# Eight weight chunks instead of six converted beside attention, and one conversion stage of the MLP less

## The chip, the cores and the metric

The kernel runs on one core of one Trainium2 chip. The metric is device time in microseconds (us). Each time comes from one execution; a kernel is timed several times, and one further execution is recorded by the hardware profiler. The engines work side by side, each through its own instructions in their order: PE (TensorE: matmuls, and PEld, its weight loads), DVE (VectorE), ACT (ScalarE), POOL (GpSimd), and SP (SyncE), whose queue issues most DMAs.

## The reference

The program is attention with a causal mask and a decay bias, followed by a block that mixes tokens by a Fourier transform and ends in an MLP. Cut to what matters:

```python
# q, k, v: 8 batches x 8 heads x 576 tokens x 64; s: 8 x 8 x 576
scores = scale * np.matmul(q, k.transpose(0, 1, 3, 2))
cum = np.cumsum(np.maximum(s, 0.0), axis=-1)
bias = -(cum[:, :, :, None] - cum[:, :, None, :])
scores = np.where(causal, -1e9, scores + np.minimum(bias, 0.0))
attn = softmax(scores)
x = heads joined(attn @ v)                      # 8 x 576 x 512
u = x + np.real(np.fft.fft(np.fft.fft(x, axis=1), axis=2))
un = (u - mean(u)) / np.sqrt(var(u) + 1e-6)
out = u + np.maximum(un @ w_ch1, 0.0) @ w_ch2   # 512 x 2048, 2048 x 512
```

The two weight matrices arrive as 64-bit floats, seen by the kernel as pairs of 32-bit words. They have to be rounded to 32-bit floats on the chip, and are then split into a high and a low part, since a product is made of three matmuls on such parts.

## The kernel before

**Attention.** The loop in fused_kernel runs over 32 head pairs i (8 batches of 4 pairs). In iteration i several generators are woven together by weave, which always goes on with the stream that has the least of its total behind it: scores(i) (matmuls of L491 and L492, exponentials of L495 on ACT), av(i - 1) (attention times values, L523), maxes(i + 1), and loads, casts and the finishing of other pairs. maxes(i + 1) is a chain that comes back to PE: low writes the low part of k on DVE (L435), matmuls on L459 write pm, ten reductions on DVE (L466, two helped by L462) leave the row maxima in Mx, PE transposes Mx (L471), ACT copies it, and a DMA puts it into KQ, from which scores(i + 1) starts. The pm tiles and the results of av share five PSUM buffers.

From the second half of each fourth pair on, folds and fourier run for the batch that has been finished, woven into the next batch's attention. The last batch's transform runs inside the first part of the MLP.

**Weights.** There are 16 chunks f of 128 x 1024 weights. A chunk is converted in four quarters by rounded: a DMA of 256 KB brings raw (L78), DVE takes exponent and mantissa apart (L83, L85), ACT shifts the exponent (L84), DVE puts in the sign and the low bits (L87, L88), POOL multiplies the two (L89). The first NC = 6 chunks are converted beside attention by convert_w, which keeps one set of buffers and writes each quarter (128 KB) to DRAM as wD. In each iteration the stream take(weights, share) may go on by share, where a quarter costs 0 + 0.4 + 0.4 + 0.2 by its yields; take stops after the step that reaches the share. For chunks below NC, load_w later reads all 512 KB from wD into wl (L107), copies wl to wh on ACT (L112), and subtracts (L114: the first half on DVE, the second on POOL). For the other chunks load_w converts on the spot, in buffers of a pool named stage.

**MLP.** The 4608 tokens are nine tiles of 512. mlp_tile runs over the chunks: twelve matmuls make h (L183), ACT and DVE make zh and zl of it (L187, L188), and twelve matmuls add the chunk before into acc (L196 to L198). All weights stay in SBUF, so only the first tile waits for them. They come from the generator rest: chunks 3 to 7 into pool w1, converted in stage1 (4 sets of buffers) where they aren't in wD; then it runs the last batch's fourier to its end, closes the pool of the Fourier tables, and in its memory opens wB and stage2 (3 sets) for chunks 8 to 15. The stream ahead draws from rest as the first tile goes on, and mlp_tile draws from it when a chunk two ahead is missing.

**Order.** In attention and its tail the order on PE is the order of the program text (manual_schedule), up to order.close() before the MLP. All else is put in order by a scheduler.

Of the kernel before, what the change touches and what calls it, by code (L numbers as in the profile page):

```python
# [24 lines left out]
NF = FF // 128  # L25
NEG = -1.0e30
TOK = 512
NC = 6
NC1 = 4.5
N0 = 3  # L30
N1 = 8
WEXP = 0x38000000 + (20 << 20)
# [9 lines left out]
def fused_kernel(ctx, tc, qkT, vA, sP, wP, tabD, tabS, corr, out):  # L42
# [3 lines left out]
    NP = NB * 4  # L46
# [27 lines left out]
    def rounded(pool, f, x, bufs):  # L74

        m = pool.tile([128, WC], I32, tag="wm", name="wm", bufs=bufs)
        raw = pool.tile([128, 2 * WC], I32, tag="raw", name="raw", bufs=bufs)
        nc.sync.dma_start(out=raw, in_=wP[f, :, WC * x:WC * x + WC].bitcast(I32))  # L78
        hi = raw.rearrange("p (n w) -> p n w", w=2)[:, :, 1]
        lo = raw.bitcast(U16).rearrange("p (n w) -> p n w", w=4)[:, :, 1]  # L80
        yield 0.0
        e = pool.tile([128, WC], I32, tag="we", name="we", bufs=bufs)
        nc.vector.tensor_scalar(e, hi, 0x7FF00000, None, op0=ALU.bitwise_and)  # L83
        nc.scalar.activation(e, e, AF.Relu, bias=wbias, scale=8.0)  # L84
        nc.vector.tensor_scalar(m, hi, 0xFFFFF, 0x100000, op0=ALU.bitwise_and, op1=ALU.bitwise_or)  # L85
        yield 0.4
        nc.vector.scalar_tensor_tensor(out=e, in0=hi, scalar=-0x80000000, in1=e, op0=ALU.bitwise_and, op1=ALU.bitwise_or)  # L87
        nc.vector.scalar_tensor_tensor(out=m.bitcast(F32), in0=lo, scalar=2.0 ** -16, in1=m, op0=ALU.mult, op1=ALU.add)  # L88
        nc.gpsimd.tensor_mul(e.bitcast(F32), m.bitcast(F32), e.bitcast(F32))  # L89
        yield 0.4  # L90
        return e.bitcast(F32)

    def convert_w(pool, lo, hi, bufs):

        for f in range(lo, hi):
            for x in range(1024 // WC):
                m = yield from rounded(pool, f, x, bufs)
                nc.sync.dma_start(out=wD[f, :, WC * x:WC * x + WC], in_=m)
                yield 0.2

    def load_w(pool, f):
# [3 lines left out]
        W[f] = (wh, wl)  # L105
        if f < NC:
            nc.sync.dma_start(out=wl.bitcast(F32), in_=wD[f])  # L107
        n = 512 if f < NC else WC
        for x in range(1024 // n):
            xs = slice(n * x, n * x + n)  # L110
            m = wl[:, xs].bitcast(F32) if f < NC else (yield from rounded(stage, f, x, nstage))
            nc.scalar.copy(wh[:, xs], m)  # L112
# [287 lines left out]
    def load(i):  # L400
        b, j = divmod(i, 4)
        qk = atop.tile([128, 2, S], F32, tag="qk", name="qk", bufs=3)
        nc.sync.dma_start(out=qk, in_=qkT[b, j])
        kq = KQ[i % NR]
        sts[i] = dict(b=b, j=j, qy=kq[:, 1], ky=kq[:, 0, :, 0:S], kq=kq, qk=qk)
# [100 lines left out]
    def av(i):  # L506
        st = sts[i]
        va = st["va"]
        x = attb.tile([128, S], F32, tag="stage", name="stage", bufs=3)
        r1 = rows[32 + 32 * (i % 2):33 + 32 * (i % 2)]  # L510
        sums = attb.tile([32, 36], F32, tag="sums", name="sums", bufs=2)
        for h in range(2):
            P = st["P"][h]
            vs = slice(64 * h, 64 * h + 128)
            for lo, n, tg in ((0, 256, "A"), (256, 320, "B")):
                p = psm.tile([128, 512], F32, tag="m", name="pav" + tg, bufs=5)
                cs = [c for c in range(5) if CH[c][3] < lo + n]
                for c in cs:
                    qk = CH[c][3]
                    a = max(lo, qk)  # L520
                    o = POFF[c] + a - qk
                    w = lo + n - a
                    nc.tensor.matmul(p[:, a - lo:n], va[:, c, vs], P[:, o:o + w], start=c == 0, stop=c == cs[-1])  # L523
                    if c == cs[-1]:
                        if h:
                            nc.scalar.copy(r1[:, lo:lo + n], p[0:1, :n])
                            nc.scalar.copy(x[64:128, lo:lo + n], p[64:128, :n])  # L527
                        else:
                            nc.scalar.copy(x[:, lo:lo + n], p[:, :n])
                    yield 4 * w / 2.4  # L530

            nc.sync.dma_start(out=sums[16 * h:16 * h + 16], in_=r1 if h else x[64:65])
        st.update(x=x, sums=sums)
# [41 lines left out]
    mixing = None  # L575
    weights = convert_w(attb, 0, NC, 1)
    tiles = [(t, min(TOK, NT - t)) for t in range(0, NT, TOK)]
    stage_ctx = ExitStack()

    def pool(name, **kw):  # L580
        return tc.tile_pool(name=name, bufs=1, reuse_waits="tile", **kw)
# [3 lines left out]
    for i in range(NP):  # L585
        if i + 3 < NP:
            load(i + 3)
        streams = []
        if i >= 1:
            streams.append([av(i - 1), AV * (0.95 if i % 4 == 1 else 1.0)])  # L590
        if 2 <= i + 1 < NP:
            streams.append([maxes(i + 1), MAXES / 0.7])
            streams.append([later(low(i + 1), i % 4 == 0), (6, 7, 4, 3)[i % 4]])
        if 3 <= i + 2 < NP:
            streams.append([high(i + 2), 6])
        if i == 2:
            load_tables()
        if i >= 2:
            streams.append([later(call(recip, i - 2), 4), 10])
            streams.append([later(call(finish, i - 2), 6), 10])  # L600
        if i >= 6 and i % 4 == 2:
            b = (i - 6) // 4
            folding = folds(b, *xbuf[b])
            streams.append([later(take(folding, 5), 2), 7 / 0.7])
        if i >= 7 and i % 4 == 3:
            streams.append([folding, FOLDS - 5])
        if mixing is not None:
            quota, pace = MIX[i % 4]
            streams.append([take(mixing, FOURIER * quota), FOURIER * pace])
        share = NC1 * 4.0 / (NP - 2) if i < NP - 2 else (1.0, 4.0)[i - NP]  # L610
        streams.append([take(weights, share), share + 1e-9])
        if i == NP - 1:
            atop_ctx.close()
            lnp = ctx.enter_context(pool("lnp"))
            mlps = [ctx.enter_context(pool("mlp0"))]
            norm = ln_tile(*tiles[0], 6)
            streams.append([take(norm, 10), 10 / 0.9])
        streams.append([scores(i), SCORES * (1.1 if i % 4 == 1 else 1.0)])
        weave(*streams)
        if i >= 7 and i % 4 == 3:  # L620
            mixing = fourier(b, *xbuf.pop(b))
# [5 lines left out]
    stage, nstage = attb, 1  # L627
# [5 lines left out]
    weave([folds(b, *xbuf[b]), 1.0])  # L633
    mixing = fourier(b, *xbuf.pop(b))
    attb_ctx.close()
    stage, nstage = stage_ctx.enter_context(pool("stage1", side="right")), 4
    w1 = ctx.enter_context(pool("w1"))
    accp = ctx.enter_context(pool("accp", space=PSUM))
    order.close()
# [56 lines left out]
def later(gen, n):  # L696
    for _ in range(n):
        yield 1.0
    yield from gen
# [113 lines left out]
```

## Time and profile before

| | us |
|---|---|
| three timed runs | 1424.47, 1429.97, 1430.12 (median 1429.97) |
| profiled execution, its own time | 1426.1 |
| its span, from the first to the last instruction | 1424.4 |
| PE busy | 1305.1 (92%) |
| DVE busy | 745.7 (52%) |
| POOL busy | 561.6 (39%) |
| ACT busy | 539.3 (38%) |
| mean granted clock of TensorE | 0.971 |

How to read the profile: the page gives busy times of the engines over the span and a chain of waits. A table by stretches cuts the span into pieces and gives, for each, its limits and length, then the busy time of PE, PEld, DVE, ACT and POOL with the number of instructions as (xN), then granted clock, DMA share and GB/s. A group of instructions has line, engine, operation, output<-input, shape and count, then busy time and mean ns of one, then the idle time of its engine before them and what ended it. A timeline row has start and duration in us, engine, line, operation, and in square brackets how long the engine had been idle and who released it. PE's recorded matmuls overlap, so a busy PE isn't yet a PE at its peak.

### The profile page before, as it was taken

What the parts mean: (1) busy time and instruction counts of PE and PEld (TensorE: products, weight loads), DVE (VectorE), ACT (ScalarE), POOL (GpSimd) and SP (SyncE); (2) the same over time, 40 slices, a digit from 0 to 9 for tenths busy, and PEclk for the clock granted to TensorE, in tenths of its full rate; (3) what the DMA queues carried; (4) which work ended last, traced back from release to release, by engine and by line L of the source; (5) the groups of instructions that cost most, each with busy time, mean ns of one, the idle gap of its engine ahead of it and who ended that gap; (6) DMA issues with size and microseconds to landing.
All of it is one profiled execution on the core that took longest, in us unless ns stands there. A gap on an engine that the chain in (4) does not pass through costs nothing.

```text
span 1424.4 us, 17997 instructions
## 1 busy us (share of the span) xinstructions
PE 1305.1 (92%) x6190; PEld 1068.7 (75%) x6190; DVE 745.7 (52%) x1684; ACT 539.3 (38%) x1211; POOL 561.6 (39%) x543
## 2 busy tenths in 40 slices
PE   4887979897988887997899999999999999999998
PEld 3766868686777676775688888888888888888886
DVE  6667677877777788799833233222332223322212
ACT  4775756676665656344321121211212112121110
POOL 6445465656546566565720402204022040123300
PEclk9998999999999997999899999999999999999999
DMA  8555556565655555433200000000000000000000
GB/s 214 156 159 144 163 149 180 158 168 159 159 161 144 166 149 163 162 123 121 79 8 30 31 30 15 15 30 31 30 15 15 30 30 30 15 16 0 30 0 30
DMA packets 78230, 125.05 MB, mean 88 GB/s; under 512 B 11256, under 2 KB 36249, under 8 KB 78139
## 3 DMA queue, kind: packets, MB, share of 16 engines
q1 hardware_dynamic: 75627, 119.83, 28.4%
q0 software_dynamic: 1696, 2.50, 0.9%
q10 hardware_dynamic: 816, 1.57, 0.3%
q8 instruction: 49, 0.80, 0.2%
q14 instruction: 42, 0.34, 0.1%
HBM read 76.85 MB, written 23.07 MB: 70 GB/s over the span
## 4 chain that ended last, share of the span: by engine, by line
PE 51%; DVE 7%; POOL 2%; DMA 1%; issue 1%; ACT 1%; SPq 0%; DVEq 0%; POOLq 0%; ACTq 0%
PE h L183 25%; PE acc L198 8%; PE acc L196 8%; PE acc L197 8%; POOL we L89 1%; DVE wm L88 1%; DVE we L83 1%; DVE wm L85 1%; DVE we L87 1%; DVE wl L114 1%; ACT wh L112 1%; DMA wl<-wD 0%; POOL wl L114 0%; DVE ucl L148 0%; DVE zl L188 0%
## 5 line engine op out<-in xcount | busy, mean ns | idle before, releaser
L188 DVE SCALAR_TENSOR_TENSOR zl<-h,zh 128x512 fp32r<-128x512 f32 x144 | 98.6, 686 | 405.5 <-ACT zh L187 405.4
L187 ACT ACTIVATE zh<-h 128x512 fp32r<-128x512 f32 x144 | 85.9, 596 | 530.1 <-PE h L183 530.1
L198 PE MATMUL acc<-zl,wh 128*128 128x512 f32 x576 | 227.5, 396 | 4.9 <-DVE zl L188 4.9
L196 PE MATMUL acc<-zh,wh 128*128 128x512 f32 x576 | 227.6, 395 | 1.0 <-ACT zh L187 1.0
L197 PE MATMUL acc<-zh,wl 128*128 128x512 f32 x576 | 226.8, 394 | 0.0
L523 PE MATMUL pavB<-P,va 128*128 128x320 f32 (+2 forms) x640 | 189.1, 389 | 9.5 <-ACT stage L527 8.9
L459 PE MATMUL pm<-KQ 128*128 128x256 f32 (+3 forms) x384 | 156.5, 427 | 44.4 <-DVE Mx L466 23.1
L495 ACT ACTIVATE P<-ps 128x320 f32<-128x320 f32 (+4 forms) x384 | 145.9, 393 | 110.5 <-PE ps L492 106.8
L491 PE MATMUL ps<-KQ 128*128 128x256 f32 (+2 forms) x384 | 154.1, 404 | 24.4 <-ACT P L495 14.0
L183 PE MATMUL h<-uch,wh 128*128 128x512 f32 x576 | 159.9, 398 | 8.3 <-ACT wh L112 8.3
L183 PE MATMUL h<-uch,wl 128*128 128x512 f32 x576 | 158.1, 396 | 0.8 <-DVE wl L114 0.8
L183 PE MATMUL h<-ucl,wh 128*128 128x512 f32 x576 | 156.9, 393 | 0.0
L466 DVE CUSTOM_DVE_ANT_0 trash<-pm,amask 128x128 bf16<-128x128 f32 (+3 forms) x256 | 123.5, 482 | 34.2 <-PE pm L459 16.9
L212 POOL TENSOR_TENSOR o<-o,w 128x512 f32<-128x512 f32 x32 | 41.8, 1305 | 252.3 <-issue 218.5
L183 PEld LDWEIGHTS h<-uch,wh 128*128 128x128 f32 x576 | 108.2, 190 | 35.9 <-ACT wh L112 12.1
L198 PEld LDWEIGHTS acc<-zl,wh 128*128 128x128 f32 x576 | 108.7, 189 | 32.0 <-DVE zl L188 6.9
L183 PEld LDWEIGHTS h<-uch,wl 128*128 128x128 f32 x576 | 109.2, 190 | 26.6 <-DVE wl L114 1.2
L196 PEld LDWEIGHTS acc<-zh,wh 128*128 128x128 f32 x576 | 108.6, 188 | 26.1 <-ACT zh L187 1.8
L183 PEld LDWEIGHTS h<-ucl,wh 128*128 128x128 f32 x576 | 108.9, 189 | 24.7
L197 PEld LDWEIGHTS acc<-zh,wl 128*128 128x128 f32 x576 | 108.6, 189 | 24.7
L459 PEld LDWEIGHTS pm<-KQ 128*128 128x128 f32 x384 | 78.4, 207 | 64.7 <-DVE Mx L466 30.2
L492 PE MATMUL ps<-q,k 128*128 128x256 f32 (+2 forms) x384 | 120.5, 316 | 3.1 <-POOL q L438 3.1
(140 smaller groups left out, 2066.9 us busy)
## 6 DMA issues: line engine op xcount, KB each, us to landing
qk<-in_qkT_dram SPq DMA_DIRECT2D x32, 576.0 KB
raw<-in_wP_dram SPq DMA_DIRECT2D x64, 256.0 KB
va<-in_vA_dram SPq DMA_DIRECT2D x32, 480.0 KB
q<-KQ SPq DMA_DIRECT2D x32, 288.0 KB
k<-KQ SPq DMA_DIRECT2D x32, 288.0 KB
rb<-rd SPq DMA_DIRECT2D x64, 144.0 KB
u<-uD SPq DMA_DIRECT2D x8, 1024.0 KB
out_dram<-o SPq DMA_DIRECT2D x32, 256.0 KB
```

The source lines that it names most:

```text
L183: nc.tensor.matmul(h[:, :n], a[:, j * 128:(j + 1) * 128], b[:, j, :n], start=i == 0, stop=i == 11)
L187: nc.scalar.activation(zh[:, :n], h[:, :n], AF.Relu)
L188: nc.vector.scalar_tensor_tensor(out=zl[:, :n], in0=h[:, :n], scalar=0.0, in1=zh[:, :n].bitcast(F32), op0=ALU.max, op1=ALU.subtract)
L196: nc.tensor.matmul(acc[j][:, :n], a[:, cs], y[:, :n], start=g == 0, stop=False)
L197: nc.tensor.matmul(acc[j][:, :n], b[:, cs], y[:, :n], start=False, stop=False)
L198: nc.tensor.matmul(acc[j][:, :n], a[:, cs], z[:, :n], start=False, stop=g == NF - 1)
L459: nc.tensor.matmul(p[:, :n], qy[:, h, 128 * c:128 * c + 128], ky[:, h, k0:k0 + n], start=True, stop=True)
L466: nc.vector.tensor_tensor_reduce(out=trash[:nq, :n], in0=p[:nq, :n], in1=amask[:nq, m0:m0 + n], scale=1.0, scalar=first if x else NEG, op0 ...
L491: nc.tensor.matmul(p[:, :n], ky[:, h, ksl], qy[:, h, a:a + n], start=True, stop=False)
L492: nc.tensor.matmul(p[:, :n], k1[:, h, ksl], q1[:, h, a:a + n], start=False, stop=True)
L495: nc.scalar.activation(P[:, o:o + a + n - lo], p[:, lo - a:n], AF.Exp, scale=0.125)
L523: nc.tensor.matmul(p[:, a - lo:n], va[:, c, vs], P[:, o:o + w], start=c == 0, stop=c == cs[-1])
```

## The change

NC goes from 6 to 8, so chunks 6 and 7 are also converted beside attention and read from wD. Up to pair 6 the share is 1.6 a pair; in pairs 7 to 29 it is 4.0 * 4 / (30 - 7) = 0.696 (before, 4.5 * 4 / 30 = 0.6 in all of pairs 0 to 29); the shares of the last two pairs stay 1.0 and 4.0. Nothing is left to convert in w1, so stage1 goes.

```diff
-NC = 6
-NC1 = 4.5
+NC = 8
+NEARLY = 7
+NC1 = 4.0
...
-        share = NC1 * 4.0 / (NP - 2) if i < NP - 2 else (1.0, 4.0)[i - NP]
+        share = (1.6 if i < NEARLY else NC1 * 4.0 / (NP - 2 - NEARLY)) if i < NP - 2 else (1.0, 4.0)[i - NP]
         streams.append([take(weights, share), share + 1e-9])
...
     attb_ctx.close()
-    stage, nstage = stage_ctx.enter_context(pool("stage1", side="right")), 4
+    stage, nstage = None, 0
     w1 = ctx.enter_context(pool("w1"))
```

One line is added near the top, so lines of the changed kernel are one higher from there on (L466 becomes L467).

On DVE, in the fourth head pair of attention, the maxima of pair 4 stood in one piece before (k is the low part of k, trash and Mx belong to the maxima, sums to another pair's row sums):

```order
L435 TENSOR_TENSOR k_670<-qk,KQ_120 64x576 x2
L466 ISA trash,Mx_128<-pm,amask 128x128
L466 ISA Mx_128 128x1
L466 ISA trash,Mx_128<-pm,amask 128x256
L466 ISA Mx_128 128x1
L466 ISA trash,Mx_128<-pm,amask 128x384
L466 ISA Mx_128 128x1
L466 ISA trash,Mx_128<-pm,amask 128x512
```

At the same place two quarters of a chunk (we, wm and raw are their tiles) now stand among them:

```order
L436 TENSOR_TENSOR k_710<-qk,KQ_120 64x576 x2
L467 ISA trash,Mx_128<-pm,amask 128x128
L467 ISA Mx_128 128x1
L84 TENSOR_SCALAR we<-raw 128x256
L86 TENSOR_SCALAR wm<-raw 128x256
L89 SCALAR_TENSOR_TENSOR wm<-raw,wm 128x256
L88 SCALAR_TENSOR_TENSOR we<-raw,we 128x256
L467 ISA trash,Mx_128<-pm,amask 128x256
...
L84 TENSOR_SCALAR we<-raw 128x256
L86 TENSOR_SCALAR wm<-raw 128x256
L467 ISA trash,Mx_128<-pm,amask 128x512
```

The maxima behind them move back by four and by eight instructions. The pattern is the same in the pairs around it; from pair 7 on there is one quarter a pair, after three to five maxima, and from pair 26 on none.

On PE, at the start of the first token tile, the last batch's transform (pzc, pzs, pyc, pys and p) came in pieces between the chunks, and its last matmul stood behind chunk 5 (wh_6615):

```order
L183 MATMUL h<-uch,wh_6615 128x512 x4
L183 MATMUL h<-uch,wl_6616 128x512 x4
L183 MATMUL h<-ucl,wh_6615 128x512 x4
...
L284 MATMUL pzs<-dsin_81,Do_6509 96x256
...
L336 MATMUL p_6968<-scos_83,z_92 4x290
L183 MATMUL h<-uch,wh_6622 128x512 x4
```

Now all of it but its first six matmuls stands in one piece between chunk 3 and chunk 4 (wh_6664):

```order
L293 MATMUL pzc<-dcos_79,De_6595 97x258
...
L285 MATMUL pzs<-dsin_81,Do_6597 96x256
...
L337 MATMUL p_6909<-scos_83,z_92 4x290
L184 MATMUL h<-uch,wh_6664 128x512 x4
L184 MATMUL h<-uch,wl_6665 128x512 x4
L184 MATMUL h<-ucl,wh_6664 128x512 x4
```

The end of the transform, and with it the memory for chunks 8 to 15, comes two chunks earlier in PE's order.

In SP's queue, behind the last batch's DMAs (xs, rows), three chunks were read from wD and the first fourteen quarters of raw were issued before the transform's results (uD):

```order
L107 DMA wl_6573<-wD 128x1024
L107 DMA wl_6580<-wD 128x1024
L107 DMA wl_6616<-wD 128x1024
L78 DMA raw<-in_wP_dram 128x512 x14
L328 DMA uD<-xs 128x576
L327 DMA uD<-xa 128x2x576
```

Now five chunks are read there, and six quarters follow:

```order
L108 DMA wl_6658<-wD 128x1024
L108 DMA wl_6665<-wD 128x1024
L108 DMA wl_6701<-wD 128x1024
L108 DMA wl_6708<-wD 128x1024
L108 DMA wl_6744<-wD 128x1024
L79 DMA raw<-in_wP_dram 128x512 x6
L329 DMA uD<-xs 128x576
```

The eight quarters of chunks 6 and 7 are gone from here, and two reads of 512 KB from wD have taken their place.

## The prediction

> **What bounds the kernel now.** I read the page first, whose chain of waits runs mostly over PE, then cut the span into four stages with the table by stretches, since a mean over stages with different limits says little.
>
> ```profile
> core 0: us, PE busy (x) PEld busy (x) DVE busy (x) ACT busy (x) POOL busy (x), PEclk, DMA share, GB/s
> 0.00:523.40 523.40, 439.73 (x2439) 369.46 (x2440) 379.63 (x1097) 327.87 (x805) 296.03 (x318) 0.95 0.59 162
> 523.40:572.40 49.00, 38.07 (x181) 31.44 (x180) 41.01 (x70) 29.59 (x69) 33.33 (x29) 0.79 0.52 167
> 572.40:702.50 130.10, 110.99 (x474) 85.44 (x473) 116.59 (x247) 56.13 (x125) 77.54 (x84) 0.95 0.36 122
> 702.50:1424.40 721.90, 716.27 (x3102) 582.40 (x3100) 208.42 (x272) 125.73 (x213) 154.73 (x115) 1.00 0.06 23
> ```
>
> The rows are attention up to the last transposition of maxima, its tail up to the first matmul of the MLP, the first token tile, and the other eight tiles. In the last row PE is busy 99% and nothing else half as much: the change can't touch it. In the first tile DVE is busy 90%, PE 85%. There the chain and PE's timeline show what PE waits for:
>
> ```profile
> 711.80 2.80 PE h L183 x12
> 717.36 2.80 PE h L183 x12
> ...
> 666.59 0.73 PE L183 MATMUL h<-uch,wh 128*128 128x512 f32 x2 [1.65 <-ACT wh L112]
> 675.40 0.74 PE L183 MATMUL h<-uch,wh 128*128 128x512 f32 x2 [1.40 <-ACT wh L112]
> 684.29 0.73 PE L183 MATMUL h<-uch,wh 128*128 128x512 f32 x2 [0.87 <-ACT wh L112]
> ```
>
> In later tiles a chunk (twelve matmuls of h, twelve of acc) takes 717.36 - 711.80 = 5.56 us. In the first tile the last chunks begin 8.8 and 8.9 us apart, and each waits for wh, the converted weights. Why conversion is so slow is in the groups of DVE from 624 to 702.5:
>
> ```profile
> L87 DVE SCALAR_TENSOR_TENSOR we<-raw,we 128x256 int32<-128x256 int32 x29 | 16.4, 571 | 0.4 <-ACT we L84 0.2
> L88 DVE SCALAR_TENSOR_TENSOR wm<-raw,wm 128x256 f32<-128x256 uint16 x28 | 15.3, 547 | 0.5
> L83 DVE TENSOR_SCALAR we<-raw 128x256 int32<-128x256 int32 x29 | 12.2, 424 | 0.0
> L85 DVE TENSOR_SCALAR wm<-raw 128x256 int32<-128x256 int32 x27 | 10.9, 403 | 0.0
> L114 DVE TENSOR_TENSOR wl<-we,wh 128x256 fp32r<-128x256 f32 x16 | 8.0, 505 | 1.9 <-ACT wh L112 1.8
> L188 DVE SCALAR_TENSOR_TENSOR zl<-h,zh 128x512 fp32r<-128x512 f32 x10 | 6.8, 680 | 0.4 <-ACT zh L187 0.4
> ```
>
> One quarter of a chunk costs DVE 0.571 + 0.547 + 0.424 + 0.403 = 1.95 us. A chunk is four of these, two wl and one zl: 7.8 + 1.0 + 0.7 = 9.5 us, against PE's 5.56. The first tile is bound by DVE's conversions.
>
> **The change, term by term.** Times are against the profiled execution's own 1426.1 us.
>
> Where the quarters go. A quarter's steps cost 0, 0.4, 0.4 and 0.2, and take stops at the step that reaches the share. Counting this out: through pair 6 before has 4.75 quarters, after 13.5 (+8.75); pairs 7 to 24 have 12 and 18 (+6); pairs 25 to 30 have 4.25 and 0.5 (-3.75); pair 31 has 3 and none. Together +8.
>
> (1) First seven pairs, 1.25 quarters more each. Four of their windows, from one transposition of maxima to the next, and how DVE runs in one:
>
> ```profile
> 47.10:60.50 13.40, 11.75 (x67) 9.60 (x66) 8.92 (x30) 8.26 (x21) 4.20 (x7) 1.00 0.55 129
> 60.50:73.40 12.90, 11.90 (x67) 9.82 (x66) 8.71 (x26) 8.99 (x24) 6.68 (x8) 1.00 0.55 159
> 90.20:103.60 13.40, 11.66 (x66) 9.74 (x65) 10.15 (x30) 10.32 (x26) 6.38 (x8) 1.00 0.45 138
> 103.60:117.10 13.50, 12.06 (x67) 9.82 (x66) 10.05 (x27) 8.26 (x22) 8.03 (x8) 1.00 0.60 150
> ...
> 92.36 1.86 DVE L435 TENSOR_TENSOR k<-qk,KQ 64x576 fp32r<-64x576 f32 x2 [3.19 <-PE ps L492]
> 94.47 1.18 DVE L83 TENSOR_SCALAR we<-raw 128x256 int32<-128x256 int32 x1
> 103.37 0.07 DVE L466 DVE_READ_ACCUMULATOR2_ANT Mx<- 64x1 f32 x1
> ...
> L471 PE MATMUL pmt<-ident,Mx x1: 272/272/272, 103.6 to 103.6; 128*10 128x128 f32 x1
> ```
>
> The first and third window hold one quarter (30 instructions on DVE against 26 and 27), the others none: 13.40 against a mean of 13.20, so a first quarter costs about 0.2 us and 1.25 of them 0.25. DVE has 3 to 4.5 us free in each window, which is the cover. But it isn't free at any place: DVE waits 3.19 us for the scores of the pair before until it may write k, then does ten maxima, and the order puts both new quarters between them. The last maximum ends at 103.44 and the transposition starts at 103.6. Behind it in PE's fixed order stand the rest of the scores, which let the next k start. So little of DVE's free time lies behind the maxima, and if none does, 1.25 quarters cost their whole DVE time. That time shows in a quarter that nothing disturbs, by its first and last row:
>
> ```profile
> 80.23 0.40 DVE L83 TENSOR_SCALAR we<-raw 128x256 int32<-128x256 int32 x1
> 81.25 0.42 DVE L87 SCALAR_TENSOR_TENSOR we<-raw,we 128x256 int32<-128x256 int32 x1
> ```
>
> It is 81.67 - 80.23 = 1.44 us, which makes 1.8 us a pair. I take the middle of 0.25 and 1.8, **1.0 us a pair, +7.0**; ends +1.8 and +12.6. The DMAs of these quarters (256 KB in, 128 KB out) go through SP's queue ahead of KQ, va and qk, which are loaded one to three pairs ahead; a DMA share of 0.45 to 0.60 leaves room, and I cost them at nothing. Without that cover a late KQ stops the maxima as a whole.
>
> (2) The rest of attention, +6 and -3.75, net 2.25 quarters. Whole batches of four pairs:
>
> ```profile
> 139.10:207.30 68.20, 58.17 (x337) 49.39 (x336) 50.47 (x145) 43.01 (x109) 38.65 (x41) 0.95 0.56 156
> 207.30:271.70 64.40, 57.78 (x336) 49.02 (x335) 48.63 (x141) 42.86 (x107) 38.80 (x40) 0.97 0.55 155
> 271.70:340.30 68.60, 59.17 (x337) 50.95 (x336) 49.40 (x145) 43.70 (x109) 38.75 (x42) 0.93 0.61 174
> 340.30:408.00 67.70, 59.26 (x346) 50.34 (x345) 50.87 (x147) 43.35 (x108) 40.22 (x41) 0.97 0.58 161
> 408.00:474.50 66.50, 58.21 (x337) 49.82 (x336) 48.83 (x141) 43.17 (x107) 39.58 (x40) 0.97 0.53 150
> ```
>
> A quarter is four instructions on DVE: batches with three quarters (145 and 147) take 68.2 on average, with two (141) 65.5: at most 2.7 us a quarter, though two batches of one kind already differ by 2.1. The lower end is the 0.2 of (1). I take 0.9, nearer to the lower end: **+2.0**; ends +0.5 and +6.1.
>
> (3) The tail loses its quarters. PE's waits there:
>
> ```profile
> 528.21 0.38 PE L491 MATMUL ps<-KQ 128*128 128x256 f32 x1 [2.12 <-ACT P L495]
> 530.60 0.58 PE L491 MATMUL ps<-KQ 128*128 128x256 f32 x1 [0.91 <-ACT P L495]
> 566.95 0.61 PE L306 MATMUL pyc<-scos,zc 96*128 96x290 f32 x1 [2.25 <-DVE z L299]
> ```
>
> The sum is 5.3 us. The first two fall where ACT's step of a quarter stands among the exponentials, and the third behind a quarter's L87 on DVE. But folds and the reciprocals of the sums stand in the same queues, stay, and are late next: **-3.0**; ends 0 and -5.3.
>
> (4) The first tile, with PE's rows around the last Fourier transform.
>
> ```profile
> 593.30 0.36 PE L284 MATMUL pzs<-dsin,Do 128*96 128x256 f32 x1 [0.88 <-DVE Do L70]
> 596.48 1.07 PE L183 MATMUL h<-uch,wh 128*128 128x512 f32 x4
> ...
> 611.66 0.95 PE L284 MATMUL pzs<-dsin,Do 128*96 128x256 f32 x6 [1.72 <-DVE zl L188]
> 613.09 0.97 PE L292 MATMUL pzc<-dcos,De 128*96 128x258 f32 x6 [0.48 <-DVE zs L70]
> ```
>
> Chunks 6 and 7 come as DMAs of 512 KB instead: 8 x 1.95 = 15.6 us less of DVE. But DVE can't use this at once, since chunk 8 needs memory of the last Fourier transform. The order moves that on PE from behind chunk 5 to behind chunk 3, two steps of 5.56 = 11.1 us earlier. From there the eight conversions left are the same work on DVE and on the path. Its inputs are there: the last fold (Do) had come when PE went on at 593.30, and chunk 4 began at 596.48, where the transform will go on. So 11.1 us come from the move, and I add 0.9 for waits that PE had in it on a fuller DVE (1.72 on zl, 0.48 on zs): **-12.0**. Ends: -15.6 if all DVE time counts, and -8 if the transform, now without chunks between its steps, waits 3 to 4 us more for its splits on ACT and DVE.
>
> The sum: 7.0 + 2.0 - 3.0 - 12.0 = -6.0, so 1420.1 on the scale of the profiled execution. The three runs shown (1424.5, 1430.0, 1430.1) and it average 1.6 higher than it, which makes **1422 us**. 0.5%, about what a measurement of this kernel can tell from no change, is 7.1 us.
>
> **Rivals.**
>
> A. Forecast: conversion moves to a cheaper place, and attention gives back most of it. 1422, within 1415 to 1428. Chance 0.42.
>
> B. The second quarter of a pair costs what the first does. For it: 3 to 4.5 us of DVE idle in each window. Against it: where that idle time lies. 1.8 + 0.5 - 3.0 - 12.0 = -12.7, 1415. Chance 0.25.
>
> C. Slower: the maxima on DVE become the bound of the early pairs. Two quarters in one pair mean two more multiplies on POOL, and what DVE does beside POOL is long. The two of L435 took 1.86 us in the row above, but 3.71 in the next pair:
>
> ```profile
> 105.25 3.71 DVE L435 TENSOR_TENSOR k<-qk,KQ 64x576 fp32r<-64x576 f32 x2 [1.81 <-PE ps L492]
> 117.10:139.10 22.00, 14.80 (x67) 11.62 (x66) 17.96 (x43) 12.44 (x30) 11.24 (x12) 0.77 0.61 163
> ```
>
> Quarters at the first tile's 1.95 us make 2.4 us a pair; a pair in which PE then stands still runs at a lower granted clock: in the window of the first folds it was 0.77, 14.80 x 0.23 = 3.4 us of PE's time. One such pair more is 0.5 us a pair: 7 x 2.9 = 20.3. With (2) at 6.1, (3) at -3 and (4) at -12 that is +11, 1439. It loses against before from 2.3 us a pair on at 6.1 in (2), 0.5% included. Chance 0.17.
>
> The Trainium skill, in "SBUF — State Buffer", section "Who interferes with whom", says that a DVE instruction with two SBUF inputs and a GpSimd instruction take one shared port pair as an exclusive lock, the later one blocked until the other ends. The two rows of L435, 1.86 and 3.71 for two, agree with it, though no row names the lock. By it each added multiply could hold DVE once: at the 0.93 us that each L435 lost, 8.75 of them come to 8.1 us, and the sum to +2.1 instead of -6.0. Of the clock, "TensorE: Matmul & The Clock Gate", Part 1, says that an idle window of about 3.4 us halves it; the 0.77 agrees, and this too speaks against placing much in one pair.
>
> D. The change doesn't reach what it aims at: five weight DMAs now stand in SP's queue ahead of the raw chunks, or DVE is as late with the transform's splits as with quarters, and the conversions start only 4 us earlier. 7.0 + 2.0 - 3.0 - 4.0 = +2, 1430. Chance 0.16.
>
> **From these to the numbers.** Faster by over 0.5%: B, and two fifths of A (0.17): 0.42. Within 0.5%: the rest of A (0.25) and most of D (0.14): 0.39. Slower: C and the rest of D: 0.19. The range goes from 1407 (B with (3) and (4) at their lower ends is 1409, less 2 for the scatter of runs) to 1436 (D with (1) at 12.6), and leaves out the worse part of C.
>
> **What would show it.** (1): windows of the early pairs at 14 to 15 us, with PE's transposition waiting for DVE's Mx; at 13.5 B holds, at 16 C. (2): batches near 69 us, and the last six pairs shorter than before. (3): first h of the MLP about 3 us earlier against pair 31. (4): the last matmul of L337 (L336 before) followed by chunk 4, some 10 to 12 us earlier after the first h; first tile near 118 us instead of 130; DVE still its bound. The forecast is wrong if the early pairs cost over 2 us each, or if chunk 8's conversion doesn't follow the transform.

## The result, and the profile after

The changed kernel takes 1468.14 us (median of 4 runs, 1465.38 to 1470.44) against 1430.05 of the kernel before (4 runs, 1424.47 to 1430.9). The ratio is 1.0273 (95% interval 1.0248 to 1.0298): **slower by 2.7%**, and outside the predicted range of 1407 to 1436. The profiled execution took 1470.44 us, its span is 1468.7 us (1424.4 before), its mean granted clock 0.957 (0.971).

The table by stretches of the kernel after, at the same four cuts as before (lines are one higher than before):

```profile
0.00:572.80 572.80, 460.48 (x2439) 384.82 (x2440) 396.00 (x1144) 330.36 (x816) 304.69 (x330) 0.92 0.57 156
572.80:619.70 46.90, 37.06 (x181) 31.89 (x180) 35.35 (x55) 27.69 (x65) 27.87 (x26) 0.82 0.45 147
619.70:742.50 122.80, 108.66 (x475) 84.42 (x474) 106.81 (x213) 51.53 (x113) 66.33 (x73) 0.97 0.35 121
742.50:1468.70 726.20, 717.55 (x3101) 582.81 (x3099) 207.97 (x271) 125.50 (x213) 155.24 (x115) 1.00 0.06 22
```

Attention lost 49.4 us (523.4 to 572.8), the tail won 2.1, the first tile 7.3, and the other tiles lost 4.3, of which 4.0 lie in the first two chunks of the second tile. Together +44.3, the whole difference of the spans (the medians of the times differ by 38.1: the profiled run of before was 4.0 below its median, that of the change 2.3 above). Everything hangs on the first row. Inside it, the pairs 2 to 7 and 8 to 27, first before, then after:

```profile
47.10:139.10 92.00, 75.76 (x392) 61.71 (x391) 66.77 (x185) 59.29 (x146) 45.32 (x49) 0.93 0.57 153
139.10:474.50 335.40, 292.58 (x1686) 249.52 (x1685) 248.19 (x719) 216.09 (x538) 196.00 (x202) 0.96 0.57 159
```

```profile
47.10:173.90 126.80, 88.42 (x392) 71.50 (x391) 75.44 (x221) 62.87 (x157) 51.42 (x57) 0.83 0.52 135
173.90:527.50 353.60, 301.71 (x1685) 254.58 (x1684) 261.18 (x739) 216.31 (x542) 198.89 (x207) 0.94 0.56 160
```

+34.8 us in the six pairs 2 to 7, which hold nine quarters more (36 instructions on DVE), and +18.2 in the pairs 8 to 27, which hold five more (20 instructions). The pairs 28 to 30, with fewer, won 3.6. In the early pairs DVE is busy 75.4 of 126.8 us, so its work is not their bound: PE stands still 22.2 us longer than before (38.4 against 16.2) and its busy time is 12.7 us longer at a granted clock of 0.83 instead of 0.93, with the same 392 matmuls.

What waits there shows in the view of waits for the pairs 2 to 7 (total us, times, longest), here PE, DVE and SP's queue of the kernel after:

```profile
PE pm L460 <- DVE Mx L467: 27.5, 9, 6.7
...
DVE we L84 <- DMA raw<-in_wP_dram: 18.2, 7, 3.6
DVE k L436 <- PE ps L493: 11.6, 5, 3.2
DVE sums L539 <- DMA sums<-rows: 10.5, 4, 3.1
...
SPq L99 <- POOL we L90: 35.3, 10, 7.5
```

The same three engines before:

```profile
PE pm L459 <- DVE Mx L466: 3.6, 2, 2.6
...
DVE k L435 <- PE ps L492: 11.8, 4, 4.6
DVE sums L538 <- DMA sums<-rows: 0.8, 1, 0.8
...
SPq L98 <- POOL we L89: 2.6, 2, 1.5
```

PE's 24 us more of waiting for maxima stand against 28 us more in which DVE, with those maxima behind it in its queue, waits for loads of two kinds, raw and sums. One such wait, in the rows of DVE, SP's queue and PE around 95 us:

```profile
90.84 0.42 DVE L88 SCALAR_TENSOR_TENSOR we<-raw,we 128x256 int32<-128x256 int32 x1
94.31 0.17 DVE L539 TENSOR_SCALAR sums<-sums 32x36 f32<-32x36 f32 x1 [1.99 <-DMA sums<-rows]
97.55 0.29 DVE L84 TENSOR_SCALAR we<-raw 128x256 int32<-128x256 int32 x1 [2.67 <-DMA raw<-in_wP_dram]
97.96 0.68 DVE L467 CUSTOM_DVE_ANT_0 trash<-pm,amask 128x512 bf16<-128x512 f32 x1
```

```profile
92.11 0.35 SPq L99 DMA_DIRECT2D wD<-we  x1
92.56 0.58 SPq L533 DMA_DIRECT2D sums<-rows  x1
93.24 0.54 SPq L79 DMA_DIRECT2D raw<-in_wP_dram  x1
```

```profile
93.61 0.31 PE L493 MATMUL ps<-q,k 128*128 128x320 f32 x1
98.71 0.58 PE L460 MATMUL pm<-KQ 128*128 128x256 f32 x1 [4.79 <-DVE Mx L467]
```

The first quarter of the pair reads raw until 91.26. Its write (L99) waits at the head of SP's queue for POOL's multiply, until 92.08. Only then go the sums and the raw of the second quarter, which is there 4.3 us after its issue. DVE comes to the second quarter at 94.9 and stands until 97.55, and PE until 98.71. Before, a raw was issued at 43.03 and read at 50.80, without a wait:

```profile
43.03 0.36 SPq L78 DMA_DIRECT2D raw<-in_wP_dram  x1
...
50.80 0.29 DVE L83 TENSOR_SCALAR we<-raw 128x256 int32<-128x256 int32 x1
```

### The profile page after: what moved, and what is told of

Its sections match the earlier page's. It is cut to its first block, busy times and chain, and to the rows that moved or that the text cites. A ratio compares the mean times of both kernels' runs of the same rounds, so it can differ in the third digit from the quotient of the medians.

```text
span 1468.7 us, 17999 instructions
## 1 busy us (share of the span) xinstructions
PE 1323.7 (90%) x6190; PEld 1083.9 (74%) x6190; DVE 746.1 (51%) x1682; ACT 535.1 (36%) x1207; POOL 554.1 (38%) x541
## 4 chain that ended last, share of the span: by engine, by line
PE 50%; DVE 7%; issue 1%; POOL 1%; ACT 1%; DMA 0%; SPq 0%; DVEq 0%; POOLq 0%; ACTq 0%
PE h L184 24%; PE acc L199 8%; PE acc L197 8%; PE acc L198 8%; DVE wl L115 1%; DVE we L84 1%; DVE wm L86 1%; DVE we L88 1%; DVE wm L89 1%; POOL we L90 0%; DVE u L147 0%; DVE zl L189 0%; DVE ucl L149 0%; PE pys L316 0%; PE pyc L307 0%
## 5 line engine op out<-in xcount | busy, mean ns | idle before, releaser
L460 PE MATMUL pm<-KQ 128*128 128x256 f32 (+3 forms) x384 | 166.3, 452 | 63.6 <-DVE Mx L467 51.2
L524 PE MATMUL pavB<-P,va 128*128 128x320 f32 (+2 forms) x640 | 196.3, 402 | 2.2 <-ACT stage L528 2.2
L492 PE MATMUL ps<-KQ 128*128 128x256 f32 (+2 forms) x384 | 157.6, 412 | 28.0 <-ACT P L496 12.0
L184 PE MATMUL h<-uch,wh 128*128 128x512 f32 x576 | 156.9, 394 | 0.0
L460 PEld LDWEIGHTS pm<-KQ 128*128 128x128 f32 x384 | 82.9, 219 | 86.0 <-DVE Mx L467 60.5
L467 DVE CUSTOM_DVE_ANT_0 trash<-pm,amask 128x128 bf16<-128x128 f32 (+3 forms) x256 | 123.4, 482 | 29.5 <-PE pm L460 15.7
```

The lines of the kernel that those rows point to most:

```text
L184: nc.tensor.matmul(h[:, :n], a[:, j * 128:(j + 1) * 128], b[:, j, :n], start=i == 0, stop=i == 11)
L460: nc.tensor.matmul(p[:, :n], qy[:, h, 128 * c:128 * c + 128], ky[:, h, k0:k0 + n], start=True, stop=True)
L467: nc.vector.tensor_tensor_reduce(out=trash[:nq, :n], in0=p[:nq, :n], in1=amask[:nq, m0:m0 + n], scale=1.0, scalar=first if x else NEG, op0 ...
L492: nc.tensor.matmul(p[:, :n], ky[:, h, ksl], qy[:, h, a:a + n], start=True, stop=False)
```

## The experiments

Where no interval is given, a time is that of one execution. How far equal stretches scatter is seen in five runs whose edits lie in the first tile alone: pairs 2 to 7 took 126.8 to 129.7 us in four copies of the changed attention and 91.7 to 93.6 in three of the one before, pairs 8 to 27 took 351.4 to 355.2 and 335.4 to 339.1 (the two kernels included). Between the means of these copies the change costs 35.6 and 16.0 us there.

### What an early quarter costs, and by what

e1 spreads the quarters evenly:

```diff
-NEARLY = 7
-NC1 = 4.0
+NEARLY = 0
+NC1 = 7.5
```

> The change with an equal share of 1.0 in each of the first 30 pairs, so one quarter a pair instead of two in the first seven; the MLP is as in the change. Theory R (the reload): what costs in the early pairs is a second quarter in the same pair, whose raw can be loaded only when the first has been read, and whose load and write stand in SP's queue ahead of the sums; with one quarter a pair the windows of pairs 2 to 6 fall from 18.5-23.4 us to 14-15.5, pair 31's transposition comes at 525 to 550 instead of 572.8, and the run takes 1425 to 1450. Theory W (the work): a quarter costs the same wherever it stands; the attention still holds some 31 quarters, and the run stays within 10 us of 1468.

1479.68 us, slower than the change. Both theories miss. In the pairs 2 to 7 (first row) much of the crowd's price is gone, 104.1 instead of 126.8 us, though the windows of pairs 2 to 6 (13.6 to 18.1) are mostly longer than R's. And one quarter a pair in the later pairs cost far more than R allowed.

```profile
46.50:150.60 104.10, 79.30 (x391) 62.33 (x390) 68.23 (x193) 58.99 (x147) 45.41 (x50) 0.93 0.54 141
150.60:533.20 382.60, 309.78 (x1685) 257.35 (x1684) 269.20 (x747) 218.23 (x547) 200.53 (x210) 0.92 0.53 147
```

e2 loads raw one quarter ahead, into a second buffer (cut):

```diff
+            if n + 1 < len(todo):
+                raws[todo[n + 1]] = fetch(pool, *todo[n + 1], 2)
-                m = yield from rounded(pool, f, x, bufs)
+            m = yield from rounded(pool, f, x, bufs, raws.pop((f, x)))
```

> The change, with the raw of a quarter loaded one quarter ahead into a second buffer; the same quarters in the same pairs, the same work on every engine. Theory R: DVE's 18.2 us of waiting for raw in the pairs 2 to 7 goes, and PE's 27.5 us of waiting there for the maxima falls to 10 to 15; the waits for the sums (10.5 us) stay, since the write of a quarter still stands in SP's queue ahead of them. Windows of pairs 2 to 6 at 15.5 to 19, the run 1445 to 1458. Theory W (DVE's and POOL's work and their port): nothing changes, windows of 18.5 to 23.4 and 1468.

e3 issues the write from POOL's queue:

```diff
-                nc.sync.dma_start(out=wD[f, :, WC * x:WC * x + WC], in_=m)
+                nc.gpsimd.dma_start(out=wD[f, :, WC * x:WC * x + WC], in_=m)
```

> The change, with the write of a converted quarter to memory issued from POOL's queue, behind the multiply that makes it, instead of SP's. Theory R: SP no longer stands 35.3 us in the pairs 2 to 7 for POOL's multiply, so the sums' DMAs and the next raw are issued earlier; the 10.5 us for the sums goes and the 18.2 us for raw falls by about a third; windows of pairs 2 to 6 at 16 to 19, the run 1445 to 1460, less what issuing costs POOL. Theory W: nothing changes or, with more on POOL, it gets slower, 1468 or above.

1473.62 and 1468.56 us, pairs 2 to 7 at 122.2 and 122.5: both runs end near W's numbers, not R's. The waits aimed at shrank or went (18.2 us for raw fell to 5.9 in e2), but their time hardly came back. DVE's waits in these pairs, e2 first, then e3:

```profile
DVE wm L92 <- DMA raw<-in_wP_dram: 5.9, 5, 1.9
DVE wm L92 <- POOL we L96: 5.5, 7, 0.9
DVE we L94 <- ACT we L91: 5.3, 7, 2.1
DVE we L90 <- DMA wD<-we: 3.2, 3, 1.8
```

```profile
DVE we L84 <- DMA wD<-we: 24.5, 6, 6.8
```

With raw there in time, DVE waits for the multiply, for ACT and for the write of the quarter before, which still use the tiles wm and we. With the write off SP's queue, the second quarter may not overwrite we until that write has landed. This suggests that raw was only the last link of a loop through one set of tiles: load, DVE, ACT, DVE, POOL, write.

e4 leaves conversion out of the first 30 pairs, as the zero of the scale:

```diff
-NEARLY = 7
-NC1 = 4.0
+NEARLY = 0
+NC1 = 0.0
```

> The change without conversions in the first 30 pairs; they are left to the last pairs and the tail, which grow by 50 us or more and are not compared. It prices the quarters of attention: windows of the early pairs without any quarter, and batches of four pairs without any. Theory R: 13 to 13.5 us a pair in pairs 2 to 6 and batches of 64 to 66 us, as in the windows of before that hold none, so that two quarters in a pair cost 6 us where one costs about 1. Theory W: a quarter costs some 3 us wherever it stands, so batches without any are near 59 to 62 us, since those with three took 68 to 72.

```profile
46.90:137.50 90.60, 74.44 (x392) 61.64 (x391) 60.41 (x173) 57.73 (x144) 42.36 (x44) 0.92 0.53 140
137.50:475.20 337.70, 296.33 (x1686) 253.50 (x1685) 233.08 (x667) 208.05 (x525) 188.24 (x189) 0.94 0.52 146
```

The run, with the conversions left to its end, took 1552.17 us. Without quarters the pairs 2 to 7 take 90.6 us (one quarter is left there), and 8 to 27 take 337.7: batches of 66 to 69 us, above W's 59 to 62 and a little above R's 64 to 66. So **before's 13 quarters in the pairs 8 to 27 (52 instructions more on DVE) cost nothing that can be seen** (335.4). The change's 18 cost 16 us, e1's 20 cost 45. The price is not a price of the work, so W is wrong, although e2 and e3 came out near its numbers.

e5 joins e2 with two sets of wm and we, e6 adds e3's edit, e7 takes e5 and sets a quarter's steps apart in the order, and e8 is e7 with e1's shares. The two sets, and the steps apart (cut):

```diff
-    weights = convert_w(attb, 0, NC, 1)
+    weights = convert_w(attb, 0, NC, 2)
...
+            nc.vector.tensor_scalar(e, hi, ...)
+            nc.vector.tensor_scalar(m, hi, ...)
+            yield 0.2
+            nc.scalar.activation(e, e, AF.Relu, bias=wbias, scale=8.0)
+            nc.vector.scalar_tensor_tensor(out=m.bitcast(F32), ...)
+            yield 0.2
+            nc.vector.scalar_tensor_tensor(out=e, ...)
+            yield 0.2
+            nc.gpsimd.tensor_mul(...)
+            yield 0.2
+            nc.sync.dma_start(out=wD[f, :, WC * x:WC * x + WC], in_=e.bitcast(F32))
+            yield 0.2
```

> The change with raw loaded a quarter ahead as in e2_ahead, and two sets of the tiles we and wm. In e2_ahead DVE no longer waited long for raw, but for POOL's multiply of the quarter before (4.7 us), its write (3.2) and ACT's step (4.7); in e3_wd_pool DVE waited 24.5 us for the write. Theory S (one set): what is left of the loss is this loop through one set of tiles; with two, windows of pairs 2 to 6 fall from 18.3-20.5 us to 15-16.5 and the run to 1445 to 1455. Theory O (the order): a quarter's steps stand at one place of the order, and each engine that takes them in turn (DVE, ACT, DVE, POOL, SP) stands there until the one before is done, with attention's work queued behind it; two sets change little, windows stay over 17.5 and the run over 1462. Theory W (work, and the port of DVE and POOL): as O.

> e5_two_sets with the writes issued from POOL's queue, as in e3_wd_pool, where DVE's wait for the write (24.5 us) hid what this frees. Now neither raw nor the write holds DVE, and no quarter holds SP. Theory S: 15 us a window and 1440 to 1452. Theory O: SP's stand for POOL's multiply (19.9 us in the pairs 2 to 7 of e2_ahead) goes, so some 1 us a pair better than e5_two_sets, but DVE, ACT and POOL still stand for each other: windows of 16.5 to 18, 1455 to 1465. Theory W: like e5_two_sets within 4 us.

> e5_two_sets, with the steps of a quarter set apart in the order: five steps of 0.2 (DVE's two masks; ACT and the fraction's add on DVE; DVE's sign; POOL's multiply; the write) instead of two of 0.4 and one of 0.2, so that what an engine needs was issued a piece of the order earlier. About the same quarters: 1.8 a pair in the first seven, 0.8 after. Theory O: this cures what two sets do not; windows of pairs 2 to 6 at 14 to 15.5 and batches of four pairs at 66 to 69, the run 1435 to 1448. Theory S: like e5_two_sets within 5 us. Theory W: the work is the same, so windows over 17.5 and over 1460.

> e7_staged with the equal share of 1.0 of e1_flat, one quarter in each of the first 30 pairs. In e1_flat the 20 pairs from 8 on took 382.6 us against 337.7 without quarters (e4_none), 2.2 us a quarter, while SP stood 78.6 us for POOL's multiply and POOL 50.0 for q's load behind it. Theory O: with the steps apart a quarter costs under 1 us, these pairs take 340 to 357 and the run 1430 to 1450. Theory S: one quarter a pair had a set to itself already, so 375 to 385 and 1470 to 1480. Theory W: as S.

1457.85, 1452.71, 1446.12 and 1443.7 us. The pairs 2 to 7 of e5 and of e7 (e6's took 106.8), and those of e8 with its pairs 8 to 27:

```profile
51.40:158.10 106.70, 81.67 (x391) 64.21 (x392) 77.27 (x217) 61.80 (x153) 50.27 (x55) 0.91 0.61 157
```

```profile
51.20:153.90 102.70, 80.70 (x391) 64.30 (x392) 76.08 (x213) 62.01 (x153) 49.70 (x55) 0.90 0.61 161
```

```profile
48.30:146.10 97.80, 78.55 (x391) 63.01 (x391) 69.84 (x193) 60.06 (x148) 46.72 (x49) 0.93 0.59 151
146.10:502.20 356.10, 296.12 (x1686) 249.50 (x1685) 265.67 (x747) 218.39 (x546) 199.31 (x210) 0.95 0.59 160
```

Two sets, with raw a quarter ahead, take 20 of the 36 us that the crowd cost over e4, with the same work on DVE (77.3 us against 75.4). But 4.3 of the 20 come back in the first two pairs, which now hold a quarter more and end at 51.4 instead of 47.1, so 15.8 are left. That is theory S in part: most windows (13.7 to 19.2 us) and the run lie above its numbers. Setting the steps apart takes 4 more, with about one quarter less. What is left in e7 is 12 us for some 10 quarters over e4, or 10.7 us over before for seven quarters more: 1.8 us a pair, the upper end of the prediction's (1) and not its 1.0. e7 and e8 end where O had the runs, and e8's pairs 8 to 27 took 356.1, where S had 375 to 385; but e18, below, gets under that with the steps together, so O isn't shown.

### The later pairs

e9 keeps the early pairs as before:

```diff
-        share = (1.6 if i < NEARLY else ...
+        share = (0.6 if i < NEARLY else ...
```

> The change with the share of before (0.6) in the first seven pairs and its own (0.696) behind them; some nine quarters more are left to the last pairs and the tail, which grow and are not compared. It asks of the pairs 8 to 27, which took 353.6 us in the change and 335.4 before, whether their own quarters cost this or a lateness carried over from the crowded early pairs. Theory P (the phase): at 0.696 a whole quarter falls in every pair, its write, load, masks, adds and multiply in one turn of the order, while 0.6 spreads a quarter over two pairs; the pairs 8 to 27 take 350 to 357 us again. Theory C (carried over): they take 335 to 341. Pairs 2 to 7: 90 to 94 us in both.

1441.62 us. Pairs 2 to 7 took 91.4 us, 8 to 27 took 350.7 with 20 quarters (x747): nothing is carried over from the crowd. P's number holds, though no run here tests the phase by itself. And it stands 32 us under e1, whose pairs 8 to 27 hold as many quarters:

```profile
47.00:138.40 91.40, 74.78 (x391) 60.64 (x390) 64.76 (x185) 59.02 (x146) 44.34 (x49) 0.94 0.59 154
138.40:489.10 350.70, 302.71 (x1686) 253.17 (x1685) 263.38 (x747) 220.75 (x545) 204.77 (x209) 0.95 0.57 162
```

What differs is where in a pair the steps fall. The waits of SP's queue and of POOL in the pairs 8 to 27, e1 first, then e9:

```profile
SPq L99 <- POOL we L90: 78.6, 19, 9.3
...
POOL q L439 <- DMA q<-KQ: 50.0, 11, 6.7
```

```profile
SPq L99 <- POOL P L502: 5.1, 4, 1.7
...
POOL q L439 <- DMA q<-KQ: 13.7, 5, 4.0
```

e18 asks it directly: e1 with e3's edit of one line.

> e1_flat with the write of a quarter issued from POOL's queue, behind its multiply, instead of SP's. Theory Q (SP's stand): the 78.6 us of SP and most of the 50.0 us that POOL waited for q's load go; pairs 8 to 27 take 345 to 358 us instead of 382.6 and the run 1440 to 1455. Theory O (the place of a quarter's steps on DVE, ACT and POOL): they take 372 us or more, and the run over 1468.

```profile
46.50:140.90 94.40, 76.42 (x392) 61.36 (x391) 66.45 (x193) 59.70 (x149) 50.20 (x57) 0.93 0.59 157
140.90:486.40 345.50, 293.55 (x1685) 252.67 (x1684) 268.09 (x747) 220.35 (x546) 211.92 (x229) 0.94 0.58 166
```

1437.43 us, 42 under e1: Q. The same 20 quarters now cost 7.8 us over e4 in the pairs 8 to 27 instead of 44.9. A write that waits in SP's queue for a late multiply holds the loads of all that comes next.

This is e1's price, not that of the change. In the change's pairs 8 to 27 SP's queue stood for these writes 0.7 us in three waits (the first row has two of them), and e3, with the same edit of one line, took as long there as the change (second row, against 353.6):

```profile
SPq L99 <- POOL Bw L254: 0.4, 2, 0.3
```

```profile
170.30:526.10 355.80, 297.07 (x1685) 251.90 (x1684) 268.94 (x739) 217.95 (x544) 211.36 (x226) 0.95 0.56 158
```

So what made the change's own later pairs 18.2 us longer stays open. Half of it is PE standing still (51.9 us against 42.8), half is PE's busy time (301.7 against 292.6) at a granted clock of 0.94 instead of 0.96. e6 (349.3, with 17 quarters) and e7 (347.3, with 16) got a part of it back.

e12, e7 with e3's write, puts the quarters into the first two pairs of every four, where e8's were cheap:

```diff
-        share = (1.6 if i < NEARLY else NC1 * 4.0 / (NP - 2 - NEARLY)) if i < NP - 2 else ...
+        share = (1.5 if i % 4 < 2 else 0.2) if i < NP - 2 else ...
```

> e7_staged with the writes from POOL's queue (e6_two_sets_pool) and the quarters where they were cheap: in e8_staged_flat a quarter cost -0.5 us in the first pair of four, 0.6 in the second, 2.4 in the third and 1.2 in the fourth, against the same pairs of e4_none. So 1.5 in the first two of four and 0.2 in the others. If the price goes by the place: pairs 8 to 27 at 338 to 346 us, pairs 2 to 7 at 93 to 99, the run 1424 to 1434. If the price is the number of quarters, or a second quarter in a pair costs 1.2 us more: 350 to 358, 100 to 106 and 1440 to 1450.

1463.71 us (ratio 1.0219, 1.0188 to 1.025), pairs 8 to 27 at 359.5: the price does not go by the kind of pair alone. Its second expectation is the nearer one, and even that was too low.

### The first tile

From the end of the last transform to the third chunk of the second tile, before and after:

```profile
620.50:711.60 91.10, 77.30 (x294) 58.16 (x293) 83.38 (x165) 38.59 (x84) 61.05 (x65) 0.93 0.33 112
```

```profile
619.70:657.40 37.70, 33.02 (x170) 27.20 (x169) 29.97 (x56) 13.67 (x30) 20.19 (x19) 0.95 0.41 151
657.40:755.60 98.20, 86.05 (x342) 64.95 (x341) 86.11 (x164) 40.16 (x87) 58.70 (x64) 0.97 0.30 101
```

The transform ends 37.7 us after the first h instead of 48.1, but the stretch behind it is 7.1 longer: it holds 48 matmuls more, two chunks. In the ten other runs that leave this tile as the change has it (e1 to e9 without e4, and e12 and e18) it took 97.1 to 100.3 us. Of before's tile there is this one placement alone. e10 and e11 leave out DVE's last step of a quarter for the chunks 8 to 15, in the kernel after and before (cut):

```diff
-        nc.vector.scalar_tensor_tensor(out=m.bitcast(F32), in0=lo, scalar=2.0 ** -16, in1=m, op0=ALU.mult, op1=ALU.add)
+        if not cut:
+            nc.vector.scalar_tensor_tensor(out=m.bitcast(F32), in0=lo, scalar=2.0 ** -16, in1=m, op0=ALU.mult, op1=ALU.add)
```

> The change without the last of DVE's four steps (the add of the low bits, 0.5 us) in the 32 quarters of the chunks 8 to 15, so that these weights are not the reference's: 16 us less on DVE in the first tile. From the end of the last transform to the third chunk of the second tile the change took 98.1 us. Theory D (DVE bounds it, as the prediction had it): this falls by 13 to 16 us. Theory E (PE, with two chunks more behind the transform, 14 x 5.56 = 77.8 us, bounds it nearly as much, and each waits for the other): by 4 to 9 us.

> The kernel before, with the same step left out for the chunks 8 to 15. There the stretch took 91.0 us with 12 chunks of PE's, 66.7 us. Theories D and E both: DVE bounds it, it falls by 12 to 16 us, so that under E the gain of the cut here is about twice that in e10_cut_after, and under D the same.

```profile
657.60:749.00 91.40, 83.20 (x342) 64.08 (x341) 70.40 (x136) 40.28 (x87) 54.61 (x62) 0.98 0.32 108
```

```profile
631.00:719.20 88.20, 76.07 (x294) 56.82 (x293) 71.40 (x135) 38.95 (x85) 57.94 (x63) 0.94 0.34 112
```

-6.8 and -2.9 us, with 15.7 and 12.0 us less of DVE's busy time. The first is E's, the second neither's: **DVE's work alone does not bound the tile, not even before**. Three more runs sought what does. e13 (after) and e14 (before) issue the steps of four neighbouring quarters in one step of the order (cut), e15 takes one of the three sets away:

```diff
-            yield from load_w(wB, f)
+        for t in range(len(todo) + 2):
+            fetch(t + 1)
+            first(t)
+            second(t - 1)
...
+            nc.scalar.copy(wh[:, xs], m)
```

```diff
-        stage, nstage = stage_ctx.enter_context(pool("stage2", side="right")), 3
+        stage, nstage = stage_ctx.enter_context(pool("stage2", side="right")), 2
```

> The change, with the conversions of the chunks 8 to 15 in the first tile issued a step apart: raw one quarter ahead, then the masks and ACT's step of a quarter, the second DVE step and POOL's multiply of the quarter before, and the casts of the one before that; the same instructions, still three sets. Theory O (order): ACT no longer stands for POOL (19.0 us in 18 waits) nor for DVE (15.5 in 15) with a chunk's zh behind; from the end of the transform to the third chunk of the second tile 98.2 us fall to 84 to 92. Theory T (the turn through three sets): a quarter holds its set longer, so 98 or more, to 110. Theory D (DVE's work): 96 to 100.

> The same edit in the kernel before. Theory O: its 91.1 us from the transform on fall to 78 to 86, where PE's own 12 chunks take 66.7, and the run to 1418 to 1427, faster than both kernels. Theory T: 91 to 105 us, 1430 to 1445. Theory D: 89 to 93 us, 1428 to 1433.

> The change with two sets of tiles instead of three for the conversions of the first tile, nothing else. Theory T: a chunk of 8 us is four turns of 6 us through three sets; with two it takes 12, and the 98.2 us grow by 15 to 32. Theory O or D: sets do not bound, and it grows by less than 6.

98.7, 90.0 and 99.5 us: neither order nor sets. These three lie in D's numbers, which e10 and e11 contradict. e14, hoped to beat both kernels, has a ratio of 1.002 (1.0 to 1.004). The last pair moves the multiply to DVE, in all quarters:

```diff
-        nc.gpsimd.tensor_mul(e.bitcast(F32), m.bitcast(F32), e.bitcast(F32))
+        nc.vector.tensor_mul(e.bitcast(F32), m.bitcast(F32), e.bitcast(F32))
```

> The change, with the multiply of every quarter, L90, on DVE instead of POOL. Theory L (DVE loses time while POOL works): DVE's masks in the first tile fall from 0.53 us to 0.35 or less, which pays for the 0.42 of the multiply, and the 98.2 us from the end of the transform to the third chunk of the second tile fall to 88 to 95. Theory D+E (work): 32 x 0.42 = 13 us more on DVE, 101 to 108. In the early pairs POOL no longer stands for a quarter, nor P's masks behind it, but the one set of tiles stays: windows of pairs 2 to 6 at 16.5 to 20 us if POOL's stand counts there, 18.5 to 23.4 if only the set does.

> The same edit in the kernel before. Theory L: its 91.1 us fall to 81 to 88 and the run to 1419 to 1428, faster than both kernels. Theory D+E: 95 to 104 and 1435 to 1445.

94.8 us (98.2) and 98.5 (91.1), the whole runs 1462.52 us and a ratio of 1.0102 (1.0044 to 1.016): L's side in one kernel, D+E's in the other. DVE's masks did get shorter: by the groups of DVE in the first tile, L84 took 516 ns in the mean after and 361 in e16. The rows of DVE and POOL of the kernel after show what held them:

```profile
694.01 0.83 DVE L84 TENSOR_SCALAR we<-raw 128x256 int32<-128x256 int32 x1
696.09 0.29 DVE L84 TENSOR_SCALAR we<-raw 128x256 int32<-128x256 int32 x1
```

```profile
693.84 0.85 POOL L90 TENSOR_TENSOR we<-wm,we 128x256 f32<-128x256 f32 x1 [1.02 <-DVE we L88]
696.32 0.84 POOL L90 TENSOR_TENSOR we<-wm,we 128x256 f32<-128x256 f32 x1 [1.63 <-DVE we L88]
```

The first mask starts while a multiply of POOL is under way, and ends 0.15 us after it; the second starts before the multiply and isn't held. Of the 64 masks (L84 and L86) in the change's first tile 29 took 0.50 us or more, each of them started beside a running instruction of POOL, and each ended 0.15 us after that one. In e16 it is 8 of 64.

What sets the pace of the first tile stays open: PE and DVE are each busy 88% of the 98.2 us, and taking work from the one, order or buffers gives back only a part. The early pairs of e16 took 123.1 us with POOL's multiply gone, and their windows (18.2 to 21.5) span both of its expectations there, so POOL's own work was at most a small part of what held them.

## Why the prediction was wrong

The forecast was -6.0 us on the profiled span; it became +44.3.

- **(1), the first seven pairs: +7.0 (ends +1.8, +12.6), measured +34.8. This step failed**, and over half of the miss is here, 27.8 of 50.3 us. It priced a quarter by DVE's 1.44 us and said of the DMAs through SP's queue "I cost them at nothing", with a late KQ as the only danger. What came late was the raw of a pair's second quarter, the last link of the loop: with one set of tiles it can't be loaded until the first has been read, and the tiles behind it come free later still. e5, with raw ahead and two sets, got back 15.8 us by the end of these pairs, and e7's steps apart 4 more; for the rest no run names the cause. Before, a quarter had a lead of 7.8 us from issue to read (43.03 to 50.80), and the prediction did not ask what gave it. The lead is gone once the quarters come in twos.
- **(2), the rest of attention: +2.0 (to +6.1), measured +14.6** (+18.2 and -3.6). This step failed too: it went by the number of quarters. Before, its 13 quarters were free there (e4); e9 and e1 hold 20 each and lie 32 us apart, which e18 puts down to e1's writes at the head of SP's queue. In the change those writes hardly stood, and moving them gave nothing (e3), so the cause of its own +18.2 stays open.
- **(3), the tail: -3.0, measured -2.1.** Right.
- **(4), the first tile: -12.0 (ends -8, -15.6), measured -3.3** with the start of the second tile. The move came as said: the transform ends 10.4 us earlier after the first h, against the 10 to 12 foretold. The step "from there the eight conversions left are the same work on DVE and on the path" failed. Behind the transform PE now has 14 chunks instead of 12, 14 x 5.56 = 77.8 us instead of 66.7, and DVE's work alone was not the bound (e10, e11); what was stays open. In the ten other placements with this tile unedited, first h to the second tile's third chunk took 133.4 to 137.8 us, against 139.2 before: the exchange is worth 1.4 to 5.8 us.

Of the rivals, C had the sign with 0.17, but by another mechanism (DVE as the bound, 20.3 us): DVE was idle for 51 of the 126.8 us. Its price for a pair that makes PE stand, a slower clock, is in the rows: 0.83 granted in pairs 2 to 7, and after the wait of 4.79 us a pm of 256 columns took 0.58 us, where one at 92.54, before the wait, took 0.28. D had the 4 us of the first tile, not for its reasons. The section "Who interferes with whom" of "SBUF — State Buffer" in the Trainium skill has the port lock also for tensor_scalar, where it runs in a mode that uses both ports: whoever issues first holds the pair for its whole instruction. The 29 masks that ended 0.15 us after POOL agree with it, though no row names the mode. But this was not what cost the early pairs: nine quarters more added 8.7 us to DVE's busy time there (66.8 to 75.4), less than 1.44 each, and with POOL's multiply gone, at 0.44 us a quarter more on DVE, the pairs came down by 3.7 us only (126.8 to 123.1).

No version beat the kernel before. The best with eight chunks, e18, lies 6.6 us above its neighbour run of before (1437.43 and 1430.8). Against the profiled run of before its span is 11.3 us longer: its last transposition of maxima comes 9.8 us later (533.2 against 523.4), the tail takes 1.9 more, the first tile with two chunks of the second gives 1.4 back, and the rest takes 1.0 more.

## What to carry to other kernels

Before side work is packed more densely, look up how many buffers it runs through and how long before their reads its loads are issued: a load without a wait may owe that to its sparse place alone. In an in-order DMA queue the price of a write is not its bytes but how long it stands at the head for the engine that makes its data, and who is queued behind; issuing it from that engine's own queue cost 0.58 us of POOL a write (mean of 13 in e3's pairs 2 to 7) and saved 37 us in twenty pairs of e1. It saved nothing in the same pairs of the change (353.6 and 355.8), where the write did not stand, so look first whether it does. A high busy share of one engine shows a bound only when less of its work shortens the stretch, which a run with a step left out tells.

## What the runs showed of the hardware that was not expected

- An engine at 88 to 92% busy did not bound: 12.0 us less of DVE's busy time (83.4 to 71.4) shortened a stretch of 91.1 us by 2.9.
- Busy time can hold waiting. The masks of a quarter (L84, L86) have one input in SBUF each, and took 0.28 to 0.31 us in the first tile of the change where nothing held them. The 29 of 64 that started beside a running instruction of POOL and ended 0.15 us after it took 0.50 to 1.38 us.
